# A second MoE's first product in 2x2 blocks: seven products for a pair of token tiles in place of eight

## The chip, the cores and the metric
The kernel runs on one core of a Trainium2 chip. The metric is the device time of one execution in microseconds (us), of which three runs of the kernel before were taken. A profile of one further execution shows what each engine did: TensorE (PE, with its weight loads as PEld), VectorE (DVE), ScalarE (ACT), GpSimd (POOL), and the DMA queue that SyncE issues (SP). [...]

## The reference
Linear attention without a softmax, a root-mean-square norm, and two MoE layers in a row, all in float32, on 4 x 576 = 2304 tokens of 512 channels:
```
out = q @ (k^T v) per head (8 heads of 64);  x = out / sqrt(mean(out^2) + 1e-6) * g_norm
y   = ((x @ w_a) * (x @ w_b)) @ w_out             # first MoE, d_ff 1536
h   = y @ w_in                                    # second MoE, 512 -> 1024
s   = h * softmax(h);  ln = (s - mean(s)) / sqrt(var(s) + 1e-6) * g_ln
out = ln @ w_out2                                 # 1024 -> 512
```
The weights come as float64. The change is about the product h.

## The kernel before
Each large matrix product is made of three TensorE products of rounded halves: both operands are split into a part hi that TensorE's float32 format (F32R) holds and a rest lo, and hi*hi + hi*lo + lo*hi are added up in PSUM (`three`, L562). A `group` is these three for one block of 128 along the summed axis.

**First stage.** For each of 12 slices f of 128 columns of d_ff, and each of 6 blocks j of 384 tokens, an *ab* item makes both products (24 matmuls of 384 columns), and ScalarE, VectorE and GpSimd turn them into the split gh and gl (L613 to L617); a *y* item (12 matmuls) multiplies them by w_out's slice, and VectorE adds the result to `ya`, y's sum in float32 (L657). Beside it the weights are decoded from float64 in chunks of 128 x 512 (`decode`, L275, five VectorE instructions), and `store` (L325) splits them: w_in into `winh` and `winl` with ScalarE and two GpSimd instructions a chunk, w_out2 later with g_ln's factor.

**Between the stages** `split_y` (L682) splits the whole of y into `yh` and `yl`, in the space that the first stage's x halves leave.

**Second stage**, for 18 token tiles of 128: `run_h` (L727) makes a tile's h (two banks of PSUM, a slot; 2 x 4 groups, 24 matmuls of 512 columns); `post_h` (L747) makes the softmax and the norm (reduce, exp, multiply, statistics, subtract); `run_t` (L783) transposes the result by 8 TensorE transposes and splits it into dh and dl; `run_o` (L808) is the output product (24 matmuls of 512 columns), scaled by ScalarE on the way out.

**The order** of instructions on every engine is fixed when the program is built. The class `Order` keeps a clock: `od.pe(cost, fn)` puts a TensorE piece and moves the clock on, `od.chain([...], rank, t)` puts a chain of steps on ACT ("A"), DVE ("V") and POOL ("G") as these come free by the stated costs, lower ranks first, without preemption. The engines then run in that order and wait on semaphores. Four PSUM slots of two banks each (`ps_tile`) serve ab, y, h, t and out in turn. While the first stage ends, a tile's h may run if no ab is left (L900); in the second stage a transpose goes first, then an h while fewer than four tiles are ahead of the outputs (`AHEAD`), then an output. All DMAs go through SP's queue in program order.

Of the kernel before, what the change touches and what calls it, by code (L numbers as in the profile page):

```python
# [113 lines left out]
def attention_moe_moe_kernel(ctx: ExitStack, tc, kv_in, kv_tail, q_in, g_norm, w1, w_in, w_out2, g_ln, out):  # L114
# [65 lines left out]
    extra = [("i", kt, n) for kt in range(NP) for n in range(2)] + [("o", x, 0) for x in range(3, NF2)]  # L180
# [5 lines left out]
    chunks += extra + [("o", x, 0) for x in range(3)]  # L186
# [68 lines left out]
    winh, winl, gwh, gwl, wf = {}, {}, {}, {}, {}  # L255
# [19 lines left out]
    def decode(k):  # L275
# [49 lines left out]
    def store(k, f, u, su, sf, t):  # L325

        what, x, y = k
        if what == "o" and x >= 3:
            wf[x] = w2.tile([P, CH], F32, tag=f"wf{x}", name=f"wf{x}", bufs=1)

            def keep():
                nc.gpsimd.tensor_tensor(out=wf[x], in0=f, in1=u, op=ALU.add)

            def kept(t):
                R_U.give(su)
                R_F.give(sf)
                scaled.append(x)
                decode_more()
                scale_more()

            od.chain([("G", 1.32, keep), (None, 0, kept)], rank=5, t=t)
            return
        if what == "i":
            if y == 0:
                winh[x] = w2.tile([P, DF2], F32R, tag=f"winh{x}", name=f"winh{x}", bufs=1)
                winl[x] = w2.tile([P, DF2], F32R, tag=f"winl{x}", name=f"winl{x}", bufs=1)
            hi, lo = (d[x][:, y * CH:(y + 1) * CH] for d in (winh, winl))
        elif R_WC.ok():
            hi, lo = wc[k] = take_wc(k)
        else:  # L350
            waiting.append((k, f, u, su, sf))
            return

        if what == "o":
            g = gl_sb[:, x:x + 1]
            gwh[x], gwl[x] = hi, lo
            ops = [
                ("G", 1.32, lambda: nc.gpsimd.tensor_tensor(out=f, in0=f, in1=u, op=ALU.add)),
                ("A", 0.6, lambda: nc.scalar.activation(out=hi, in_=f, func=AF.Copy, scale=g)),
                ("V", 0.66, lambda: nc.vector.scalar_tensor_tensor(  # L360
                    out=lo, in0=f, scalar=g, in1=hi.bitcast(F32), op0=ALU.mult, op1=ALU.subtract)),
            ]
        else:
            ops = [
                ("A", 0.58, lambda: nc.scalar.copy(out=hi, in_=f)),  # L365
                ("G", 1.32, lambda: nc.gpsimd.tensor_tensor(out=f, in0=f, in1=hi.bitcast(F32), op=ALU.subtract)),  # L366
                ("G", 1.32, lambda: nc.gpsimd.tensor_tensor(out=lo, in0=f, in1=u, op=ALU.add)),  # L367
            ]

        def done(t):  # L370
            R_U.give(su)
            R_F.give(sf)
            w_ready[k] = t
            decode_more()

        od.chain(ops + [(None, 0, done)], rank=rank_of(k) - 0.01, t=t)

    waiting, scaled = [], []

    def wc_used(k):  # L380

        R_WC.give(wc_slot[k])
        if waiting and R_WC.ok():
            store(*waiting.pop(0), od.now)
        scale_more()

    def scale_more():


        while scaled and not dec_q and not waiting:  # L390
            x = scaled[0]
            if x < 6:
                if not R_WC.ok():
                    return
                hi, lo = take_wc(("o", x, 0))
            elif ph2 is None:
                return
            else:
                hi, lo = (ph2.tile([P, CH], F32R, tag=f"gw{c}{x}", name=f"gw{c}{x}", bufs=1) for c in "hl")
# [3 lines left out]
    def scale(x, hi, lo):
        f, g = wf[x], gl_sb[:, x:x + 1]
        gwh[x], gwl[x] = hi, lo

        def done(t):
            w_ready["o", x, 0] = t

        od.chain([  # L410
            ("A", 0.6, lambda: nc.scalar.activation(out=hi, in_=f, func=AF.Copy, scale=g)),
            ("V", 0.66, lambda: nc.vector.scalar_tensor_tensor(
                out=lo, in0=f, scalar=g, in1=hi.bitcast(F32), op0=ALU.mult, op1=ALU.subtract)),
            (None, 0, done),
        ], rank=2)
# [208 lines left out]
    def y_items(fs, j):  # L624
# [10 lines left out]
        def run(f, m2, i):  # L635
# [15 lines left out]
            if i == 1 and f == fs[-1]:  # L651
# [7 lines left out]
                if m2 == 1:  # L659
                    ops.append((None, 0, lambda t: y_added(f, j)))  # L660
# [8 lines left out]
    yh, yl, y_ready = {}, {}, {}  # L669
    to_split = []  # L670
    POOL_SPLIT = (3, 4)

    def y_added(f, j):
        if f == NF1 - 1:
            to_split.append(j)
            split_more()

    def split_more():
        while to_split and all((NF1 - 1, to_split[0] // 3 * 3 + i) in ab_done for i in range(3)):
            split_y(to_split.pop(0))  # L680

    def split_y(j):  # L682
        hf, c0 = j // 3, (j % 3) * NB
        if j % 3 == 0:
            yh[hf] = xs.tile([P, NP, HALF], F32R, tag=f"xh{hf}", name=f"yh{hf}")
            yl[hf] = xs.tile([P, NP, HALF], F32R, tag=f"xl{hf}", name=f"yl{hf}")
        left = [2]
        e, cost, eng = ("G", 1.96, nc.gpsimd) if j in POOL_SPLIT else ("V", 0.87, nc.vector)

        def done(t):  # L690
            left[0] -= 1
            if not left[0]:
                y_ready[j] = t
                if j == NBLK - 1:
                    second()

        for i in range(2):
            src, dh, dl = (x[hf][:, 2 * i:2 * i + 2, c0:c0 + NB] for x in (ya, yh, yl))
            od.chain([
                ("A", 0.75, lambda dh=dh, src=src: nc.scalar.copy(out=dh, in_=src)),  # L700
                (e, cost, lambda dl=dl, dh=dh, src=src: eng.tensor_tensor(
                    out=dl, in0=src, in1=dh.bitcast(F32), op=ALU.subtract)),
                (None, 0, done),
            ], rank=1)
# [17 lines left out]
    todo_h, todo_t, todo_o = list(range(NTT)), list(range(NTT)), list(range(NTT))

    def h_ready(i):
        return max([y_ready.get(i // 3, INF), ps_ready()]) if R_H.ok() else INF

    def run_h(i):  # L727
        hf, c0 = i // 9, (i % 9) * P
        slot, ps = ps_tile(f"h{i}")
        sh = R_H.take()  # L730

        def group(n, kt):
            s = slice(n * 512, (n + 1) * 512)
            three(
                ps[:, n, :], yh[hf][:, kt, c0:c0 + P], yl[hf][:, kt, c0:c0 + P],
                winh[kt][:, s], winl[kt][:, s], kt == 0, kt == NP - 1,
            )

        for n in range(2):
            for kt in range(NP):  # L740
                od.pe(G2, lambda: group(n, kt))
        if ph2 is None:
            held.append(lambda: post_h(i, slot, ps, sh))
        else:
            post_h(i, slot, ps, sh)

    def post_h(i, slot, ps, sh):  # L747
        u = ph2.tile([P, 2, 512], F32, tag="u", name=f"u{i}", bufs=5)
# [21 lines left out]
        od.chain([  # L770
# [12 lines left out]
    def run_t(i):  # L783
# [4 lines left out]
        dh = ph2.tile([P, DF2], F32R, tag="dh", name=f"dh{i}", bufs=3)  # L788
        dl = ph2.tile([P, DF2], F32R, tag="dl", name=f"dl{i}", bufs=3)
# [70 lines left out]
    while any(ab) or busy or yq:  # L860
# [3 lines left out]
        if w2 is None and not att_left[0]:  # L864
# [4 lines left out]
            w2 = tc.alloc_tile_pool(name="w2", bufs=1, side="left", reuse_waits="tile")  # L869
            decode_more()  # L870
# [17 lines left out]
        if it:  # L888
# [8 lines left out]
            split_more()  # L897
# [13 lines left out]
    while todo_o:  # L911
        od.until(od.now)
        ahead = len(todo_o) - len(todo_h)
        h_can = todo_h and h_ready(todo_h[0]) <= od.now and (ph2 is not None or len(held) < 2)
# [8 lines left out]
        if h_can and (ahead < AHEAD or not o_can):  # L923
            run_h(todo_h.pop(0))
# [72 lines left out]
```

## Time and profile before
| what | us |
|---|---|
| median of 3 runs (lowest to highest) | 731.49 (730.91 to 731.96) |
| the profiled execution, its own time | 731.34 |
| its span, from the first to the last instruction | 729.6 |
| TensorE matmuls busy in the span | 713.9 (98%) |
| VectorE, ScalarE, GpSimd busy | 492.2, 245.6, 282.7 |

The profiled execution's time is the span and 1.7 us around it. Matmuls overlap, so the duration in a row (0.39 us for 512 columns) is longer than the distance between two starts; costs of TensorE are read from starts. Idle time "<- X" was ended by X.

### The profile page before, as it was taken

The page shows a single profiled execution, that of the slowest core. Times are in us where ns is not written, and L with a number is a line of the kernel's source. Part 1 is how long each engine was busy: PE and PEld are TensorE (multiplying, and loading weights), DVE is VectorE, ACT ScalarE, POOL GpSimd, SP SyncE. Part 2 cuts the span into 40 slices and gives each one's busy share as a digit, 9 for nine tenths or more (in the row PEclk, how much of TensorE's full clock was granted, in tenths as well). Part 3 has the DMA queues.
Part 4 walks back from the last instruction along what each step waited for, and adds up shares of the span by engine and source line. Part 5 has one row for each costly group of instructions (what it writes and reads, how often), then busy time and mean ns, then how long its engine had stood idle before and what let it go on. Part 6 is the DMA issues. An engine that isn't in the chain of part 4 may idle for free.

```text
span 729.6 us, 10425 instructions
## 1 busy us (share of the span) xinstructions
PE 713.9 (98%) x4184; PEld 669.5 (92%) x4184; DVE 492.2 (67%) x674; ACT 245.6 (34%) x458; POOL 282.7 (39%) x271
## 2 busy tenths in 40 slices
PE   6889999999999999999999999999999999999998
PEld 5779999999999999999999999999878888888887
DVE  3999557797979796969694848457784453635450
ACT  4767544323333332222222222224432121222221
POOL 2876445655556464444444343222421111111010
PEclk9999999999999999999999999999999999999999
DMA  8951501121212121212121200000000000000001
GB/s 309 336 214 60 181 1 58 58 88 58 87 57 86 42 83 52 95 50 87 59 71 46 88 0 30 1 1 1 0 1 30 29 16 30 15 30 15 29 30 44
DMA packets 16336, 46.81 MB, mean 64 GB/s; under 512 B 2080, under 2 KB 3360, under 8 KB 16288
## 3 DMA queue, kind: packets, MB, share of 16 engines
q1 hardware_dynamic: 16288, 46.15, 17.8%
q8 instruction: 33, 0.54, 0.3%
q14 instruction: 15, 0.12, 0.1%
HBM read 41.42 MB, written 4.72 MB: 63 GB/s over the span
## 4 chain that ended last, share of the span: by engine, by line
PE 92%; DMA 3%; DVE 2%; ACT 1%; SPq 1%; issue 0%; ACTq 0%
PE y L644 20%; PE ab L563 13%; PE ab L564 13%; PE ab L565 13%; PE h L563 5%; PE h L565 5%; PE out L565 5%; PE out L563 5%; PE out L564 4%; PE h L564 4%; PE t L793 2%; DMA tail<-in_kv_tail 1%; PE o L491 1%; PE pkv L468 1%; DMA raw_w<-in_w 1%; PE t L533 1%
## 5 line engine op out<-in xcount | busy, mean ns | idle before, releaser
L563 PE MATMUL ab<-xh,wh_w 128*128 128x384 f32 x576 | 194.5, 338 | 0.0
L564 PE MATMUL ab<-xl,wh_w 128*128 128x384 f32 x576 | 192.6, 334 | 0.3 <-DVE xl L547 0.3
L565 PE MATMUL ab<-xh,wl_w 128*128 128x384 f32 x576 | 192.5, 334 | 0.0
L617 POOL TENSOR_TENSOR gl<-a,gh 128x384 fp32r<-128x384 f32 x72 | 77.7, 1079 | 190.4 <-ACT gh L616 190.2
L657 DVE TENSOR_TENSOR ya<-y,ya 128x768 f32<-128x768 f32 x132 | 125.2, 952 | 8.0 <-PE y L644 5.1
L563 PEld LDWEIGHTS ab<-xh,wh_w 128*128 128x128 f32 x576 | 108.2, 188 | 0.9 <-issue 0.3
L564 PEld LDWEIGHTS ab<-xl,wh_w 128*128 128x128 f32 x576 | 108.2, 188 | 0.6 <-DVE xl L547 0.6
L565 PEld LDWEIGHTS ab<-xh,wl_w 128*128 128x128 f32 x576 | 108.1, 188 | 0.0
L614 DVE TENSOR_TENSOR a<-ab,a 128x384 f32<-128x384 f32 x72 | 40.0, 555 | 88.5 <-ACT a L613 88.5
L644 PE MATMUL y<-gh,wh_w 128*128 128x384 f32 x288 | 96.9, 336 | 0.0
L644 PE MATMUL y<-gh,wl_w 128*128 128x384 f32 x288 | 96.3, 334 | 0.0
L644 PE MATMUL y<-gl,wh_w 128*128 128x384 f32 x288 | 96.2, 334 | 0.0
L613 ACT COPY a<-ab 128x384 f32<-128x384 f32 x72 | 34.4, 478 | 130.6 <-PE ab L565 130.6
L771 DVE TENSOR_REDUCE st<-h 128x1 f32<-128x1024 f32 x18 | 22.0, 1221 | 67.1 <-PE h L565 67.0
L366 POOL TENSOR_TENSOR f_w<-f_w,wh_w 128x512 f32<-128x512 f32 x36 | 48.6, 1349 | 38.1 <-ACT wh_w L365 38.1
L563 PE MATMUL h<-winh,yh 128*128 128x512 f32 x144 | 56.2, 390 | 0.8 <-DVE u L773 0.8
L565 PE MATMUL h<-winh,yl 128*128 128x512 f32 x144 | 56.2, 390 | 0.0
L564 PE MATMUL h<-winl,yh 128*128 128x512 f32 x144 | 56.1, 389 | 0.0
L644 PEld LDWEIGHTS y<-gh,wh_w 128*128 128x128 f32 x288 | 54.1, 188 | 0.3 <-issue 0.2
L644 PEld LDWEIGHTS y<-gl,wh_w 128*128 128x128 f32 x288 | 54.1, 188 | 0.0
L644 PEld LDWEIGHTS y<-gh,wl_w 128*128 128x128 f32 x288 | 54.1, 188 | 0.0
L367 POOL TENSOR_TENSOR wl_w<-f_w,u_w 128x512 fp32r<-128x512 f32 x36 | 51.7, 1436 | 1.8
(92 smaller groups left out, 1141.7 us busy)
## 6 DMA issues: line engine op xcount, KB each, us to landing
raw_w<-in_w SPq DMA_DIRECT2D x36, 512.0 KB, 3.3
kv<-in_kv SPq DMA_DIRECT2D x16, 512.0 KB, 5.2
out<-ot SPq DMA_DIRECT2D x17, 256.0 KB, 2.0
raw_i<-in_w_in SPq DMA_DIRECT2D x8, 512.0 KB, 3.3
raw_o<-in_w_out SPq DMA_DIRECT2D x8, 512.0 KB, 3.2
q<-in_q SPq DMA_DIRECT2D x12, 288.0 KB, 6.0
tail<-in_kv_tail SPq DMA_DIRECT2D x4, 256.0 KB, 6.5
q<-in_q SPq DMA_DIRECT2D x4, 192.0 KB, 4.9
```

The costliest lines, as they stand in the source:

```text
L366: ("G", 1.32, lambda: nc.gpsimd.tensor_tensor(out=f, in0=f, in1=hi.bitcast(F32), op=ALU.subtract)),
L367: ("G", 1.32, lambda: nc.gpsimd.tensor_tensor(out=lo, in0=f, in1=u, op=ALU.add)),
L563: nc.tensor.matmul(o, lhsT=ah, rhs=bh, start=first, stop=False)
L564: nc.tensor.matmul(o, lhsT=ah, rhs=bl, start=False, stop=False)
L565: nc.tensor.matmul(o, lhsT=al, rhs=bh, start=False, stop=last)
L613: ("A", 0.45, lambda: nc.scalar.copy(out=a, in_=ps[:, 0, 0:NB])),
L614: ("V", 0.5, lambda: nc.vector.tensor_tensor(out=a, in0=ps[:, 1, 0:NB], in1=a, op=ALU.mult)),
L617: ("G", 0.96, lambda: nc.gpsimd.tensor_tensor(out=gl, in0=a, in1=gh.bitcast(F32), op=ALU.subtract)),
L644: nc.tensor.matmul(o, lhsT=x[:, s], rhs=y, start=f == fs[0] and n == 0, stop=f == fs[-1] and n == 2)
L657: op = ("V", 0.87, lambda: nc.vector.tensor_tensor(out=dst, in0=src, in1=dst, op=ALU.add))
L771: ("V", 1.13, lambda: nc.vector.tensor_reduce(out=nmax, in_=ps, axis=AX.XY, op=ALU.max, negate=True)),
L793: nc.tensor.transpose(ps[:, ft * P:(ft + 1) * P], u[:, ft * P:(ft + 1) * P], ident)
```

## The change
y is cut for each pair of token tiles into 2x2 blocks (rows: the two tiles; columns: the first and second 256 channels), w_in into 2x2 blocks of 256 x 512. The pair's h is then made of seven block products P1 to P7 (Winograd's form of Strassen's method) of 6 matmuls each, of 512 columns. Four of them take sums of blocks of y (S1 to S4), four take sums of blocks of w_in (T1 to T4). The results are combined in PSUM: ScalarE copies P1 to `s1` and P5 to `s5`; VectorE adds s1 to P6 in place, P7 is accumulated on that, VectorE writes V from it and s5, P4 is accumulated on Y, P3 on P5, and VectorE adds s1 (by then overwritten with P1 + P6) to Z.

w_in's sums are made while the first stage runs (`sums`), for the first half of the channels of each block (g = 0) and then the second (g = 1); six of g = 0's seven operands are written to HBM and read back at the end of the first stage into the space of the x halves (`late_loads`). w_out2's chunks are all scaled and split when they are decoded, in their raw buffer, written to HBM and read back as well. y is not split as a whole: `ya` stays, and `make_a` makes S1 to S4 on VectorE and the splits on ScalarE and GpSimd for each pair. Rings get smaller (R_H 5 to 4, R_D 3 to 2). The diff, cut:
```diff
-    extra = [("i", kt, n) for kt in range(NP) for n in range(2)] + [("o", x, 0) for x in range(3, NF2)]
+    extra = [("i", kt, n) for k in range(2) for kt in (k, k + 2) for n in range(2)]
+    extra += [("o", x, 0) for x in range(NF2)]
...
-            R_RAW.give(slot)
+            if k[0] != "o":
+                R_RAW.give(slot)
...
+        if what == "i":
+
+            g, r = x % 2, 2 * (x // 2) + y
+            if g and len(made[0]) < 7:
+                waiting_i.append((k, f, u, su, sf))
+                return
+
+            def have(t):
+                free()
+                there[g].add(r)
+                sums(g)
+
+            od.chain([("G", 1.32, lambda: nc.gpsimd.tensor_tensor(out=bt[:, r], in0=f, in1=u, op=ALU.add)),
+                      (None, 0, have)], rank=5, t=t)
             return
...
+        if what == "o":
+
+            g = gl_sb[:, x:x + 1]
+            at = raw.bitcast(F32R)
+            hi, lo = at[:, 0:CH], at[:, CH:2 * CH]
+
+            def out_to(t):
+                free()
+                d = scr["o", x] = dr.tile([P, 2 * CH], F32, tag=f"so{x}", name=f"so{x}")
+                nc.sync.dma_start(out=d, in_=raw.bitcast(F32))
+                scr_at["o", x] = when = od.load(8 * CH * P) + 1.5
+                od.chain([(None, 0, gone)], t=when)
+
...
+            od.chain([
+                ("G", 1.32, lambda: nc.gpsimd.tensor_tensor(out=f, in0=f, in1=u, op=ALU.add)),
+                ("A", 0.7, lambda: nc.scalar.activation(out=hi, in_=f, func=AF.Copy, scale=g)),
+                ("V", 0.85, lambda: nc.vector.scalar_tensor_tensor(
+                    out=lo, in0=f, scalar=g, in1=hi.bitcast(F32), op0=ALU.mult, op1=ALU.subtract)),
+                (None, 0, out_to),
+            ], rank=5, t=t)
+            return
...
+    def sums(g):
+        b11, b12, b21, b22, ta, tb = (bt[:, i] for i in range(6))
+
+        def sub(o, a, b):
+            return ("G", 1.35, lambda: nc.gpsimd.tensor_tensor(out=o, in0=a, in1=b, op=ALU.subtract))
+
+        def pair(n, src):
+            at = wd[0 if (g, n) == (0, 6) else n + 1]
+            hi, lo = at[:, 0:CH], at[:, CH:2 * CH]
+
+            def done(t):
+                if g == 0 and n < 6:
+                    d = scr["i", n] = dr.tile([P, 2 * CH], F32, tag=f"si{n}", name=f"si{n}")
+                    nc.sync.dma_start(out=d, in_=at.bitcast(F32))
+                    scr_at["i", n] = od.load(8 * CH * P) + 1.5
+                else:
+                    bop[g, n], b_at[g, n] = (hi, lo), t
+                made[g].add(n)
+                if waiting_i and len(made[0]) == 7:
+                    for w in waiting_i:
+                        store(*w, t)
+                    waiting_i.clear()
+
+            return [("A", 0.6, lambda: nc.scalar.copy(out=hi, in_=src)),
+                    ("G", 1.35, lambda: nc.gpsimd.tensor_tensor(out=lo, in0=src, in1=hi.bitcast(F32), op=ALU.subtract)),
+                    (None, 0, done)]
+
+        parts = [
+            ({0}, lambda: pair(B11, b11)),
+            ({0, 1}, lambda: [sub(ta, b12, b11)] + pair(T1, ta)),
+            ({2}, lambda: pair(B21, b21)),
+            ({0, 1, 2, 3}, lambda: pair(B22, b22) + [sub(tb, b22, b12)] + pair(T3, tb) + [sub(b12, b22, ta)]
+             + pair(T2, b12) + [sub(ta, b21, b12)] + pair(T4, ta)),
+        ]
+        for i, (need, ops) in enumerate(parts):
+            if i not in begun[g] and need <= there[g] and (i < 3 or T1 in made[g]):
+                begun[g].add(i)
+                more = [(None, 0, lambda t: sums(g))] if i == 1 else []
+                od.chain(ops() + more, rank=5, t=od.now)
...
+    def late_loads():
+
+        for c in range(2):
+            if c not in late and all((NF1 - 1, j) in ab_done for j in range(3 * c, 3 * c + 3)) and len(made[0]) == 7:
+                late[c] = [xs.tile([P, 4 * HALF], F32R, tag=f"x{d}{c}", name=f"late{d}{c}") for d in "hl"]
+                for i, n in enumerate(((B11, T2, B21, T1), (B22, T3))[c]):
+                    at = late[c][1][:, i * 1024:i * 1024 + 1024]
+                    nc.sync.dma_start(out=at.bitcast(F32), in_=scr["i", n])
+                    bop[0, n], b_at[0, n] = (at[:, 0:CH], at[:, CH:]), max(od.load(8 * CH * P), scr_at["i", n] + 2)
+                a_more()
...
+            late["o", x] = True
+            gwh[x], gwl[x] = hi, lo
+            for c, o in enumerate((hi, lo)):
+                nc.sync.dma_start(out=o.bitcast(F32), in_=scr["o", x][:, c * CH:(c + 1) * CH])
+            w_ready["o", x, 0] = max(od.load(8 * CH * P), scr_at["o", x] + 2)
...
+            y_ready[j] = t
+            a_more()
+            if len(y_ready) == NBLK:
+                second()
...
+    R_H, R_D, R_AO = Ring(4), Ring(2), Ring(2)
...
+    AT = {"A11": 0, "A12": 1, "A22": 2, "S1": 3, "S2": 4, "S3": 5, "S4": 6}
+    SEQ = [("P1", "A11", B11), ("P6", "S2", T2), ("P2", "A12", B21), ("P5", "S1", T1), ("P7", "S3", T3),
+           ("P3", "S4", B22), ("P4", "A22", T4)]
...
+    def a_more():
+
+        while todo_a and R_AO.ok() and R_AO.taken % 2 in late and max(
+                y_ready.get(j, INF) for j in range(NBLK) if j in (2 * todo_a[0] // 3, (2 * todo_a[0] + 1) // 3)) < INF:
+            i = todo_a.pop(0)
+            make_a(i, R_AO.take(), max(y_ready[2 * i // 3], y_ready[(2 * i + 1) // 3]))
...
+    def make_a(i, slot, when):
+        at = late[slot % 2][0]
...
+        def add(o, a, b, op):
+            return ("V", 0.4, lambda: nc.vector.tensor_tensor(out=o, in0=a, in1=b, op=op))
+
+        def part(cost, d, src, last):
+            n = slice(*d)
+
+            def done(t):
+                left[0] -= 1
+                if not left[0]:
+                    a_ops[i] = t, at, slot
+
+            od.chain([
+                ("A", cost, lambda: nc.scalar.copy(out=hi[:, n], in_=src)),
+                ("G", 2.2 * cost, lambda: nc.gpsimd.tensor_tensor(
+                    out=lo[:, n], in0=src, in1=hi[:, n].bitcast(F32), op=ALU.subtract)),
+                (None, 0, done),
+            ], rank=2.5, t=max(od.now, last))
+
+        left = [4]
+        part(0.6, (0, 2), first, when)
+        part(0.35, (2, 3), a22.unsqueeze(1), when)
+        od.chain([
+            add(s[:, 0], a21, a22, ALU.add), add(s[:, 1], s[:, 0], a11, ALU.subtract),
+            (None, 0, lambda t: part(0.6, (3, 5), s[:, 0:2], t)),
+            add(s[:, 2], a11, a21, ALU.subtract), add(s[:, 3], a12, s[:, 1], ALU.subtract),
+            (None, 0, lambda t: part(0.6, (5, 7), s[:, 2:4], t)),
+        ], rank=2.5, t=max(od.now, when))
...
+    def next_h():
+
+        if not hp:
+            i = todo_h[0] // 2 if todo_h else None
+            if (i not in a_ops or R_H.taken - len(R_H.given) > 2
+                    or sum(t <= od.now for t in ps_free.values()) < 2):
+                return INF
+            return max([a_ops[i][0]] + [b_at.get((g, B11), INF) for g in range(2)])
+        p = hp[0]
+        name, _, n = SEQ[p["n"]]
+        t = max(b_at.get((g, n), INF) for g in range(2))
+        need = {"P2": "s1", "P7": "u2", "P3": "s5", "P4": "v"}.get(name)
+        return max(t, p.get(need, INF)) if need else t
...
+        name, s, n = SEQ[p["n"]]
+        (_, p1), (_, p2) = p["slots"]
+        X, Z, Y, V = p1[:, 0], p1[:, 1], p2[:, 0], p2[:, 1]
+        o = {"P1": X, "P2": X, "P5": Z, "P3": Z, "P6": Y, "P7": Y, "P4": Y}[name]
+        a = p["a"]
+        for k in range(2):
+            c = AT[s] * 256 + k * P
+            ah, al = a[:, c:c + P], a[:, c + 1792:c + 1792 + P]
+            bh, bl = bop[k, n]
+
+            first = name in ("P1", "P5", "P6")
+
+            def group():
+                for m, (x, y) in enumerate(((ah, bh), (ah, bl), (al, bh))):
+                    nc.tensor.matmul(o, lhsT=x, rhs=y, start=first and k == m == 0, stop=k == 1 and m == 2,
+                                     skip_group_check=not first)
+
+            od.pe(G2, group)
...
+        s1, s5 = bt[:, 4], bt[:, 5]
+        at = od.now + 0.2
...
+        def try_v(t):
+            if "p7" in p and "s5" in p and "v0" not in p:
+                p["v0"] = True
+                od.chain([("V", 0.69, lambda: nc.vector.tensor_tensor(out=V, in0=Y, in1=s5, op=ALU.add)), is_done("v")],
+                         rank=1, t=t)
+
+        if name == "P1":
+            od.chain([("A", 0.6, lambda: nc.scalar.copy(out=s1, in_=X)), is_done("s1")], rank=1, t=at)
+        elif name == "P6":
+            def go(t):
+                if "s1" not in p:
+                    od.chain([(None, 0, go)], t=t + 0.2)
+                    return
+                od.chain([("V", 0.69, lambda: nc.vector.tensor_tensor(out=Y, in0=Y, in1=s1, op=ALU.add)),
+                          ("A", 0.6, lambda: nc.scalar.copy(out=s1, in_=Y)), is_done("u2")], rank=1, t=t)
+            od.chain([(None, 0, go)], t=at)
+        elif name == "P5":
+            od.chain([("A", 0.6, lambda: nc.scalar.copy(out=s5, in_=Z)), is_done("s5")], rank=1, t=at)
+        elif name == "P7":
+            od.chain([is_done("p7")], t=at)
+        elif name == "P3":
+            pre = [("V", 0.69, lambda: nc.vector.tensor_tensor(out=Z, in0=Z, in1=s1, op=ALU.add))]
+            post_or_hold(p["i"], p["slots"][0], p["u"][0], pre)
+        elif name == "P4":
+            R_AO.give(p["sa"])
+            hp.pop()
+            post_or_hold(p["i"] + 1, p["slots"][1], p["u"][1], [])
+            a_more()
+
+    def post_or_hold(i, slot, sh, pre):
...
-        od.chain([
+        od.chain(pre + [
...
-        dh = ph2.tile([P, DF2], F32R, tag="dh", name=f"dh{i}", bufs=3)
-        dl = ph2.tile([P, DF2], F32R, tag="dl", name=f"dl{i}", bufs=3)
+        dh = ph2.tile([P, DF2], F32R, tag="dh", name=f"dh{i}", bufs=2)
+        dl = late[sd % 2][0][:, 3584:3584 + DF2]
...
+            wd = [w2.tile([P, 2 * CH], F32R, tag=f"wd{n}", name=f"wd{n}") for n in range(8)]
+            bt = w2.tile([P, 6, CH], F32, tag="bt", name="bt")
...
-        if todo_h and not busy and not any(ab) and len(yq) <= 2 and h_ready(todo_h[0]) <= od.now and len(held) < 2:
-            run_h(todo_h.pop(0))
+        if not busy and not any(ab) and len(todo_h) > NTT - 2 + 2 * (not hp) and next_h() <= od.now:
+            run_h()
             continue
...
-        h_can = todo_h and h_ready(todo_h[0]) <= od.now and (ph2 is not None or len(held) < 2)
+        h_can = next_h() <= od.now
...
-        if h_can and (ahead < AHEAD or not o_can):
-            run_h(todo_h.pop(0))
+        if h_can and (hp or ahead < AHEAD or not o_can):
+            run_h()
```

## Rows read from the trace of the kernel before

**Rows 1.** The page's busy times, shares and instruction counts of the engines
```profile
PE 713.9 (98%) x4184; PEld 669.5 (92%) x4184; DVE 492.2 (67%) x674; ACT 245.6 (34%) x458; POOL 282.7 (39%) x271
```

**Rows 2.** Busy time by stretch: length, then PE, PEld, DVE, ACT, POOL; granted clock
```profile
18.00:27.00 9.00, 7.01 (x74) 5.18 (x74) 8.15 (x15) 7.25 (x19) 6.75 (x5) 1.00 0.82 299
...
152.50:190.00 37.50, 37.50 (x218) 37.50 (x217) 31.55 (x44) 11.97 (x22) 20.36 (x16) 1.00 0.20 71
...
600.00:640.00 40.00, 40.00 (x191) 33.37 (x190) 20.50 (x26) 9.11 (x13) 6.58 (x15) 1.00 0.06 22
```

**Rows 3.** Groups of instructions by line and shape: busy us, mean ns of one
```profile
L563 PE MATMUL h<-winh,yh 128*128 128x512 f32 x144 | 56.2, 390 | 0.8 <-DVE u L773 0.8
```

**Rows 4.** Timeline of PE in the second stage: start, duration
```profile
602.60 0.39 PE L563 MATMUL h<-winh,yh 128*128 128x512 f32 x1
...
608.05 1.04 PE L793 MATMUL t<-ident,u 128*128 128x128 f32 x8
...
614.38 0.39 PE L563 MATMUL h<-winh,yh 128*128 128x512 f32 x1
```

**Rows 5.** Timeline of DVE in the second stage, one tile
```profile
608.32 1.22 DVE L771 TENSOR_REDUCE st<-h 128x1 f32<-128x1024 f32 x1 [5.21 <-PE h L565]
610.18 1.23 DVE L803 TENSOR_TENSOR dl<-t,dh 128x1024 fp32r<-128x1024 f32 x1 [0.63 <-ACT dh L802]
611.32 1.22 DVE L773 TENSOR_TENSOR u<-h,u 128x1024 f32<-128x1024 f32 x1
612.57 1.29 DVE L754 BATCH_NORM_STATS2 st<-u 128x6 f32<-128x512 f32 x2
...
614.14 0.75 DVE L776 TENSOR_SCALAR u<-u,st 128x1024 f32<-128x1024 f32 x1
```

**Rows 6.** Groups by line and shape, nearest in kind to the added instructions
```profile
L366 POOL TENSOR_TENSOR f_w<-f_w,wh_w 128x512 f32<-128x512 f32 x36 | 48.6, 1349 | 38.1 <-ACT wh_w L365 38.1
...
L292 DVE TENSOR_SCALAR u_w<-u_w 128x512 uint32<-128x512 uint32 x36 | 19.1, 530 | 0.3
...
L547 DVE SCALAR_TENSOR_TENSOR xl<-t,gn,xh 128x512 fp32r<-128x512 f32 x16 | 11.9, 744 | 2.1 <-ACT xh L546 1.9
...
L508 ACT COPY x<-o 128x512 f32<-128x512 f32 x16 | 9.5, 592 | 0.0
...
L292 DVE TENSOR_SCALAR u_i<-u_i 128x512 uint32<-128x512 uint32 x8 | 9.1, 1134 | 0.1
...
L547 DVE SCALAR_TENSOR_TENSOR xl<-t,gn,xh 128x256 fp32r<-128x256 f32 x4 | 1.9, 480 | 3.3 <-ACT xh L546 3.2
```

**Rows 7.** Timeline of PE at the first stage's end
```profile
508.33 0.33 PE L565 MATMUL ab<-xh,wl_w 128*128 128x384 f32 x1
...
510.58 0.39 PE L563 MATMUL h<-winh,yh 128*128 128x512 f32 x1
...
516.06 0.33 PE L644 MATMUL y<-gh,wh_w 128*128 128x384 f32 x1
```

**Rows 8.** Timeline of ACT and POOL there
```profile
509.88 0.47 ACT L613 COPY a<-ab 128x384 f32<-128x384 f32 x1
...
511.40 0.52 ACT L616 CAST gh<-a 128x384 fp32r<-128x384 f32 x1 [0.31 <-DVE a L614]
...
510.06 3.69 POOL L701 TENSOR_TENSOR yl<-ya,yh 128x768 fp32r<-128x768 f32 x2 [4.83 <-ACT yh L700]
513.68 1.04 POOL L617 TENSOR_TENSOR gl<-a,gh 128x384 fp32r<-128x384 f32 x1
```

**Rows 9.** Waits of PE, by what ended them: total us, times, longest
```profile
PE h L563 <- DVE u L773: 0.8, 1, 0.8
```

**Rows 10.** Timeline of PE at the start, two of the same product
```profile
5.48 1.12 PE L468 MATMUL pkv<-kv 128*64 128x64 f32 x16 [5.48 <-DMA kv<-in_kv]
...
23.11 0.69 PE L468 MATMUL pkv<-kv 128*64 128x64 f32 x16 [0.17 <-ACT x L508]
```

**Rows 11.** The page's DMA issues: KB each, median us from issue to landing
```profile
raw_w<-in_w SPq DMA_DIRECT2D x36, 512.0 KB, 3.3
```

More of the change, by code (lines that the diff above doesn't have):

```diff
@@ L185, in attention_moe_moe_kernel @@
             extra = extra[2:]
-    chunks += extra + [("o", x, 0) for x in range(3)]
+    chunks += extra
     a_loads = []
@@ L323, in decode, with store, free @@
         )
-    def store(k, f, u, su, sf, t):
+    def store(k, f, u, su, sf, t, slot=None, raw=None):
         what, x, y = k
[L328 to L342, printed above, removed]
-        if what == "i":
[L344 to L351, printed above, removed]
+        def free():
+            R_U.give(su)
+            R_F.give(sf)
+            decode_more()
+        if what == "i":
+            g, r = x % 2, 2 * (x // 2) + y
[8 more added lines that the diff above has]
+                      (None, 0, have)], rank=5, t=t)
             return
@@ L370, in done @@
+            return
+        if not R_WC.ok():
+            waiting.append((k, f, u, su, sf))
+            return
+        hi, lo = wc[k] = take_wc(k)
         def done(t):
-            R_U.give(su)
-            R_F.give(sf)
             w_ready[k] = t
-            decode_more()
-        od.chain(ops + [(None, 0, done)], rank=rank_of(k) - 0.01, t=t)
-    waiting, scaled = [], []
+            free()
+        od.chain([
+            ("A", 0.58, lambda: nc.scalar.copy(out=hi, in_=f)),
+            ("G", 1.32, lambda: nc.gpsimd.tensor_tensor(out=f, in0=f, in1=hi.bitcast(F32), op=ALU.subtract)),
+            ("G", 1.32, lambda: nc.gpsimd.tensor_tensor(out=lo, in0=f, in1=u, op=ALU.add)),
+            (None, 0, done),
+        ], rank=rank_of(k) - 0.01, t=t)
@@ L403, in scale @@
[L403 to L408, printed above, removed]
-        od.chain([
[L411 to L415, printed above, removed]
+    late = {}
+    def late_loads():
[7 more added lines that the diff above has]
+                a_more()
+        for x in range(NF2):
+            if ("o", x) in late or scr_at.get(("o", x), INF) > od.now:
+                continue
+            if x >= 6:
+                if 1 not in late:
+                    continue
+                at = late[1][1][:, (x - 4) * 1024:(x - 3) * 1024]
+                hi, lo = at[:, 0:CH], at[:, CH:]
+            elif any(k[0] == "w" for k in dec_q) or waiting or any(
+                    k[0] == "w" and k not in w_ready for k in list(arrived) + list(wc)) or not R_WC.ok():
+                continue
+            else:
+                hi, lo = take_wc(("o", x, 0))
+            late["o", x] = True
[3 more added lines that the diff above has]
+            w_ready["o", x, 0] = max(od.load(8 * CH * P), scr_at["o", x] + 2)
@@ L666, in y_items, with y_added @@
         ]
[L669 to L673, printed above, removed]
+    y_ready = {}
+    def y_added(f, j, t):
         if f == NF1 - 1:
[L675 to L704, printed above, removed]
+            y_ready[j] = t
+            a_more()
+            if len(y_ready) == NBLK:
+                second()
     def second():
         nonlocal ph2
-        assert not dec_q and not waiting
-        yp.release()
+        assert not dec_q and not waiting and not waiting_i
         ph1.release()
@@ L715, in second @@
         held.clear()
-        scale_more()
-    R_H, R_D = Ring(5), Ring(3)
+    R_H, R_D, R_AO = Ring(4), Ring(2), Ring(2)
     held, d_ready, dt_ready, scs = [], {}, {}, {}
     G2 = 0.68
[L722 to L741, printed above, removed]
+    todo_a, todo_h, todo_t, todo_o = list(range(NTT // 2)), list(range(NTT)), list(range(NTT)), list(range(NTT))
```

77 lines of the change are left out of this document (42 added, 35 removed).

## Prediction
> **What bounds the kernel now.** I read the page's engine shares first: PE is busy for 98% of the span, the next engine, DVE, for 67% [rows 1]. A share is an average, so I went to the stretches: in one slice of the first stage and in the second stage PE is busy all the time, at a granted clock of 1.00, while DVE has 6 us of 37.5 free in the first and half of the time in the second [rows 2]. The list of waits then has only one of PE in the second stage, 0.8 us, for a PSUM slot [rows 9]. So the time is the sum of TensorE's instructions, and what is taken from them shortens it as long as the others keep up.
>
> What one costs is read from starts. Tile after tile, a group of 24 h matmuls takes 608.05 - 602.60 = 5.45 us, 0.227 us each, transposes and output 614.38 - 608.05 = 6.33, together 11.78 us a tile [rows 4]. (The 390 ns of the grouped row [rows 3] overlap.) 18 tiles have 432 such matmuls, three groups of 144 [rows 3].
>
> **What the change removes.** Nine pairs with 7 x 6 matmuls make 378; 54 fall away, 54 x 0.227 = 12.3 us. All else on TensorE stays. From the profiled execution, 731.34 us: 719.1, if nothing new is exposed. That execution lies 0.15 us under the median, so I forecast the median by the same number.
>
> [...]
>
> **The first stage's end: +1.6 us.** Before, the wait for the last y item is filled with h: ab ends at 508.33 + 0.17 = 508.5, y of the item before runs until 510.58, then a whole h until the last y at 516.06 [rows 7]. The new condition that lets h in there is `len(todo_h) > NTT - 2 + 2 * (not hp)`: with no pair begun it reads 18 > 18, and a pair can only begin there. So nothing covers the last y. Its chain is 0.27 us from TensorE's end to the reader (an h's end 608.05 to its reduce 608.32 [rows 4, 5]), 2.04 from the copy's start to gh's end with 0.47 of that waiting for DVE, gl 1.04 [rows 8], and about 0.3 of hand-offs: 3.2 us, less y's 2.08 (510.58 - 508.5) = 1.1. gl came only at 513.68 because GpSimd was in split_y's 3.69 us [rows 8]; that goes, but make_a's splits for pair 1 are let in just then, and one of them (1.35, nearest row [rows 6]) may stand in front of gl. I take 1.6, bounds 1.1 and 3.0.
>
> **What must have arrived: 0.** Four operands are read back when the third ab of the last slice is done, three ab and y items (36 matmuls of 37.5/218 = 0.172 us each [rows 2], 6.2) ahead of the end, 18.6 us; one after another at 3.3 us each [rows 11] they need 13.2. T3, the last of the two later ones, lands 6.6 us after 508.5 = 515.1 and is read by the pair's fifth product, at about 514.2 + 4 x 1.36 = 519.6. If w_out2's loads stand ahead of them in SP's queue, it is some us late, once; that is in the range.
>
> **Pairs 0 and 1: +2.0 us.** There is no output yet to put between. After pair 0 (9.5 us) pair 1 follows; pair 0's first tile has its last product 1.36 before its end, then VectorE and ScalarE need an add 0.74, reduce 1.22, exp as long as the reduce of its shape, 1.2 (an estimate), multiply 1.25, statistics 1.57, subtract 0.75 [rows 5, 6], 6.7 alone, interleaved with the other tile's 6 and pair 1's three adds and pair 2's four sums (0.74 and 0.48 each [rows 6]). The first transpose falls into pair 1; the second and the first dl come about 1.6 us after it is over. With some 1.2 of waits inside pair 1 and less the 0.8 that PE waits there now [rows 9]: +2.0, bounds 0 and 6.
>
> **Seven later pairs: +2.5 us.** A pair has four short waits: P2 for s1's copy (0.27 + 0.59 + 0.1 = 0.96, behind P6's 1.36), P7 for add and copy (1.8, behind 2.7), P3 for s5's copy (0.96 behind 1.36), P4 for V (0.27 + 0.74 + 0.1 = 1.11 behind 1.36) [rows 4 to 6]. Undisturbed all are hidden, with 0.25 to 0.9 to spare; but DVE and ACT take what came first, and a reduce is 1.22. Its load per pair: twice 5.94 (1.22 + 1.14 + 1.25 + 1.57 + 0.75, by starts [rows 5]) = 11.9, three adds 2.2, four sums 1.9: 16.0 of 22.2 us (2 x 11.78 - 6 x 0.227), 72% in place of half. Where the order foresees a late operand it puts an output product (5.45) first, and in the steady order (pair, out, t, out, t) one or two are ready. I take 0.35 us a pair, 2.5 in all; bounds 0 and 1.2 a pair (an op of 1.22 begun just before), 8.4.
>
> The row for contention: the same VectorE instruction takes 530 ns on the first stage's weights and 1134 on w_in's chunks [rows 6], so something on the chip can double it. [...]
>
> **The first stage: 0.** w_in's eight chunks cost GpSimd 16 instructions, now 8 adds, 8 sums and 14 splits: 14 more, 19 us [rows 6], over four slices, 20.4 + 4.7 = 25.1 of 37.5 each [rows 2], 28.5 in the slice where g = 0's last four are due. [...] Scales of w_out2 (0.74 each, two a slice) come there from later. The weights' ring holds two slices, so a late chunk has a slice to catch up. SP's stores wait for splits with the weight loads behind them: same cover; DMA is used to 0.20 [rows 2]. Bounds 0 and 3.
>
> **Sum:** 731.34 - 12.3 + 1.6 + 2.0 + 2.5 = 725.1; all lower bounds 719.1 + 1.1 = 720.2, all upper ones 719.1 + 3.0 + 6 + 8.4 + 3 = 739.5, which won't meet.
>
> **Rivals.**
> *VectorE is late in every pair* (12%). [...] For it: DVE's 72% and the doubled rows. Against it: output products stand ready to fill.
>
> *PSUM slots: slower* (11%). A pair takes two of four slots at once and holds them until both softmaxes have multiplied. If the next pair comes up with one output as cover, it waits for the second tile: about 7.5 us after P4, less 5.45 = 2.0, over eight starts 16: 719.1 + 1.6 + 16 = 736.7. It decides from (12.3 - 1.6) / 8 = 1.3 us a start. For it: even now, with one slot a tile, the only wait is for a slot [rows 9]. Against: a pair's slots are held 13 and 17 us, two t 3.5 each, two outputs 6.4 each, 50 of 4 x 22.2 = 89 slot-us.
>
> *The clock falls* (2%). At the start the same product takes 1.12 us after a wait of 5.48 and 0.69 later [rows 10], though the granted clock reads full. Were PE's gaps inside pairs to do this, nine pairs at 1.62 times would add 9 x 9.5 x 0.62 = 53: 778. Against it: between 18 and 27 us PE was busy 7.01 of 9 at 1.00 [rows 2]. [...]
>
> *The first stage becomes VectorE's* (4%): each of the four w_in slices 1.5 over: 731.
>
> *As forecast* (71%): 720 to 729, faster.
>
> Within 0.2% (1.5 us) of 731.5, about what a measurement of this kernel can tell, lie half of the first rival and most of the last: faster 0.81, same 0.07, slower 0.12. The range for 8 in 10 is 720.2 to 731: the lower bounds' sum to the first rival.
>
> **What would show it.** In the second stage a steady period of about 22.5 us for two tiles with 378 h matmuls; PE idle of 1 to 3 us before the last y; PE's waits on DVE and ACT inside pairs near 0.35 us each; DVE at 70 to 80% there. I would be wrong if PE waited over 1.3 us a pair for slots or V, if PE's first-stage windows lost their 100%, or if the read-back operands were waited for.

## The result, and the profile after

| | median us | lowest to highest, runs | ratio to before, 95% |
|---|---|---|---|
| before | 731.73 | 730.91 to 732.04, 4 | |
| changed | 722.87 | 722.29 to 723.49, 4 | 0.9881 (0.9864 to 0.9898) |
| changed, once more beside before's 731.82 | 722.37 | 722.08 to 722.77, 4 | 0.9863 (0.9844 to 0.9881) |

The change takes 8.9 us off, where 6.4 were forecast (725.1 from 731.5). The page's shares first:
```profile
span 720.7 us, 10567 instructions
...
PE 701.9 (97%) x4130; PEld 658.4 (91%) x4130; DVE 522.6 (73%) x729; ACT 272.6 (38%) x515; POOL 333.1 (46%) x317
```
PE has 54 instructions less than in [rows 1], 4184 - 4130, and is still the busiest. DVE has 55 more and is busy 30 us longer in a shorter span. By stretches, with the columns of [rows 2]; the first two lie in the first stage, the others from its end on:
```profile
227.50:265.00 37.50, 37.47 (x217) 37.15 (x216) 33.69 (x49) 12.89 (x24) 23.71 (x20) 1.00 0.24 83
...
302.50:340.00 37.50, 37.47 (x216) 37.15 (x215) 33.86 (x50) 13.09 (x24) 18.62 (x16) 1.00 0.28 99
...
510.00:530.00 20.00, 18.81 (x88) 15.68 (x87) 12.14 (x16) 8.83 (x17) 8.06 (x9) 1.00 0.49 165
524.00:538.00 14.00, 12.89 (x65) 10.34 (x64) 13.88 (x20) 7.26 (x13) 6.12 (x11) 1.00 0.00 0
538.00:552.00 14.00, 14.00 (x70) 11.84 (x71) 13.87 (x20) 6.79 (x11) 6.42 (x11) 1.00 0.11 39
560.00:640.00 80.00, 80.00 (x382) 66.82 (x382) 55.47 (x83) 35.85 (x59) 29.82 (x47) 1.00 0.07 24
```
Three things are to be seen. Two windows of the first stage have a PEld that is no longer full: 0.35 us is missing in each (before, it reads 37.50 in both). From 524 to 552 DVE is busy 99% of the time. And later, 560 to 640, PE is full again while DVE is at 69%, on the average of 80 us. The waits of PE from 480 us on:
```profile
PE out L624 <- DVE lateh L945: 1.1, 1, 1.1
PE y L705 <- POOL gl L678: 1.0, 1, 1.0
PE y L705 <- ACT gh L677: 0.2, 1, 0.2
```
None of them is one of an h product. The idle time of a row is counted to the modelled end of the matmul before; what a wait costs is the distance of starts. The starts on PE around these waits, to be held against [rows 7] and [rows 9]:
```profile
509.54 0.33 PE L626 MATMUL ab<-xh,wl_w 128*128 128x384 f32 x1
...
512.20 0.45 PE L705 MATMUL y<-gh,wh_w 128*128 128x384 f32 x1 [0.24 <-ACT gh L677]
...
513.60 0.44 PE L705 MATMUL y<-gl,wh_w 128*128 128x384 f32 x1 [0.95 <-POOL gl L678]
...
535.79 1.07 PE L935 MATMUL t<-ident,u 128*128 128x128 f32 x8
537.96 0.50 PE L624 MATMUL out<-wh_o,dh 128*128 128x512 f32 x1 [1.10 <-DVE lateh L945]
```
Before, PE's one wait:
```profile
534.54 1.91 PE L793 MATMUL t<-ident,u 128*128 128x128 f32 x16
537.24 0.47 PE L563 MATMUL h<-winh,yh 128*128 128x512 f32 x1 [0.79 <-DVE u L773]
```
After, the last y item but one ends twelve matmuls after 509.71, at 511.79; the last y starts 0.41 later, its second matmul 1.23 later than due, its third 0.11: 1.74 us. Eight transposes take 0.80, so the first output was due at 536.59 and starts 1.37 late. The one wait of before costs, counted so, 1.10 (from 534.54, two times 0.80, and the h at 537.24).

A steady pair is one of 22.20 us: in the chain of work that ended last, two blocks of 42 h matmuls begin so far apart.
```profile
655.59 9.54 PE h L843 x42
...
677.79 9.54 PE h L843 x42
```

**A measure for the experiments.** The first 100 us, the attention, end at another time in each profile: its last transposes start at 99.26 and 98.89 in two profiles of before, and between 98.87 and 100.49 in eleven of the changed kernel and its variants. So besides the medians I give D, from the start of the last ab matmul (509.54) to the start of the last copy out (717.57): 208.03 us here, 208.09 in the second profile; before 218.02 and 218.03. Two profiles of one kernel differ in D by 0.06 us at most. The medians hold one more thing that D leaves out: the time outside the span is 1.7 to 1.9 us in ten of the thirteen profiles, but 2.1 in both of the changed kernel and in that of its first variant below.

### The profile page after: what moved, and what is told of

Its sections match the earlier page's. It is cut to its first block, busy times and chain, and to the rows that moved or that the text cites. A ratio compares the mean times of both kernels' runs of the same rounds, so it can differ in the third digit from the quotient of the medians.

```text
span 720.7 us, 10567 instructions
## 1 busy us (share of the span) xinstructions
PE 701.9 (97%) x4130; PEld 658.4 (91%) x4130; DVE 522.6 (73%) x729; ACT 272.6 (38%) x515; POOL 333.1 (46%) x317
## 4 chain that ended last, share of the span: by engine, by line
PE 90%; DVE 3%; DMA 3%; ACT 1%; POOL 1%; issue 1%; SPq 0%; ACTq 0%
PE y L705 20%; PE ab L624 14%; PE ab L625 13%; PE ab L626 13%; PE h L843 10%; PE out L624 5%; PE out L626 5%; PE out L625 5%; DMA kv<-in_kv 2%; PE t L935 2%; PE o L552 2%; PE pkv L529 1%; DMA tail<-in_kv_tail 1%; PE t L594 1%; ACT sq L577 0%
## 5 line engine op out<-in xcount | busy, mean ns | idle before, releaser
L678 POOL TENSOR_TENSOR gl<-a,gh 128x384 fp32r<-128x384 f32 x72 | 75.9, 1054 | 150.0 <-ACT gh L677 149.9
L718 DVE TENSOR_TENSOR ya<-y,ya 128x768 f32<-128x768 f32 x132 | 123.4, 949 | 2.8 <-PE y L705 1.0
L843 PE MATMUL h<-wd,lateh 128*128 128x512 f32 x216 | 58.6, 391 | 0.0
L677 ACT CAST gh<-a 128x384 fp32r<-128x384 f32 x72 | 36.8, 512 | 41.9 <-DVE a L675 41.3
L389 POOL TENSOR_TENSOR wl_w<-f_w,u_w 128x512 fp32r<-128x512 f32 x36 | 50.7, 1407 | 2.9 <-DVE u_w L309 1.4
L843 PEld LDWEIGHTS h<-wd,lateh 128*128 128x128 f32 x216 | 40.3, 188 | 8.3
L843 PE MATMUL h<-latel,lateh 128*128 128x512 f32 x162 | 46.3, 394 | 0.0
```

What stands on the lines that cost most here:

```text
L677: ("A", 0.45, lambda: nc.scalar.copy(out=gh, in_=a)),
L678: ("G", 0.96, lambda: nc.gpsimd.tensor_tensor(out=gl, in0=a, in1=gh.bitcast(F32), op=ALU.subtract)),
L718: op = ("V", 0.87, lambda: nc.vector.tensor_tensor(out=dst, in0=src, in1=dst, op=ALU.add))
L843: nc.tensor.matmul(o, lhsT=x, rhs=y, start=first and k == m == 0, stop=k == 1 and m == 2, skip_group_check=not first)
```

## The experiments

| kernel | median us | before beside it | ratio, 95% | D |
|---|---|---|---|---|
| pair 0 before the last y | 721.00 | 731.64 | 0.9855 (0.9840 to 0.9870) | 206.39 |
| eight products | 733.26 | 731.64 | 1.0026 (1.0016 to 1.0035) | 219.17 |
| no output within pairs | 722.63 | 731.64 | 0.9873 (0.9858 to 0.9888) | 208.32 |
| V twice, not planned | 727.08 | 731.64 | 0.9936 (0.9919 to 0.9952) | 213.09 |
| V twice, planned | 725.77 | 732.28 | 0.9912 (0.9895 to 0.9928) | 210.93 |
| dl first | 721.77 | 732.28 | 0.9859 (0.9845 to 0.9874) | 207.40 |
| both | 719.93 | 732.28 | 0.9834 (0.9819 to 0.9848) | 205.73 |
| V twice in pairs 2 to 8 | 724.11 | 731.90 | 0.9890 (0.9872 to 0.9907) | 209.72 |
| V twice in pairs 0 and 1 | 723.85 | 731.90 | 0.9884 (0.9865 to 0.9904) | 209.28 |

**Pair 0 before the last y.** The condition that can't become true is mended:
```diff
-        if not busy and not any(ab) and len(todo_h) > NTT - 2 + 2 * (not hp) and next_h() <= od.now:
+        if not busy and not any(ab) and (hp or len(todo_h) == NTT) and next_h() <= od.now:
```


> Theory A (the time is TensorE's sum; the last y item was left uncovered): with pair 0 let in before the last y, the 1.2 us of TensorE's wait there goes, 1.2 us less than the changed kernel: 721.7, no wait of y for gl in the trace. Rival B (the last y's delay is absorbed later, since VectorE bounds the first 14 us of the second stage and the first output waits for it anyway): 722.9, the wait at the first output grows from 1.1 to about 2.3 us.

D is 1.64 us shorter, and the waits of PE from 480 us on are down to one line:
```profile
PE out L624 <- DVE lateh L945: 1.1, 1, 1.1
```
P1 and P6 now stand between the last two y items. The first output's wait has not grown: theory A, with nearly the 1.74 us that starts show, not the 1.2 of the idle column. The delay was the last y's alone.

**Eight products.**
```diff
-        for k in range(2):
+        for k in (0, 1, 0, 1) if name == "P1" else (0, 1):
```


> P1 is made twice (its second run starts anew and writes the same values), so that a pair has eight products again with all the rest of the change. Theory A: 54 more matmuls of 0.227 us, +12.3 us, 735.1, some 3.4 us slower than the kernel before: that is the price of all the rest of the change. Rival B (VectorE or the waits inside pairs set the pair's pace): the added product is hidden in part, under +8 us, 731 or less.

D grows by 11.14 us. The extra product also fills time in front of the first output:
```profile
536.76 1.62 PE L843 MATMUL h<-wd,lateh 128*128 128x512 f32 x6
538.65 0.50 PE L624 MATMUL out<-wh_o,dh 128*128 128x512 f32 x1 [0.27 <-DVE lateh L945]
```
From 536.76 the six h matmuls are due to end after 1.36 us, and the output starts after 1.89, 0.53 late. In the changed kernel P4, the transposes behind it and the output are 0.26 + 1.37 = 1.63 late. So 1.1 us are filled, and the 54 matmuls cost 12.2, as worked out. By medians the kernel with eight products is 1.6 us slower than before (0.16 to 0.35%), not 3.4. Of the difference 1.1 is what the extra product fills, and 0.35 lies outside the span of the profiled runs. Rival B is out.

**No output within pairs.**
```diff
-        if o_can:
+        if o_can and not hp:
             run_o(todo_o.pop(0))
```


> No output product may start between the seven products of a pair. Theory A (pairs have no waits because an output product stands in where a product is late): TensorE waits inside most pairs, about 0.5 us each and more where a posted softmax is in front, +3 to +7 us, 726 to 730. Rival B (the pair's own products hide the copies and adds, the output in between is chance): within 1 us of 722.9.

D is 0.29 us longer, the median the same within 0.3, and the list of PE's waits is that of the changed kernel, with none at an h product. The changed kernel puts an output into three pairs (from 553.5, 617.8 and 641.4 us on). Without it P2 of pair 2 starts 0.3 us late, which is all of the 0.29; the two others lose nothing. Theory A falls but for that pair: the pair's own products hide its copies and adds.

**V twice**, first behind the planner's back, then with its knowledge:
```diff
-                od.chain([("V", 0.69, lambda: nc.vector.tensor_tensor(out=V, in0=Y, in1=s5, op=ALU.add)), is_done("v")],
-                         rank=1, t=t)
+                add_v = lambda: nc.vector.tensor_tensor(out=V, in0=Y, in1=s5, op=ALU.add)
+                od.chain([("V", 0.69, lambda: (add_v(), add_v())), is_done("v")], rank=1, t=t)
```
The second run has 1.38 in place of 0.69.


> The add that makes V runs twice in a row (the same values), and the order's clock isn't told: 0.7 us more on VectorE in each pair, and P4 has to wait for it where P3 alone stands before it (0.25 us to spare by the working of the prediction). Theory A (hidden with little to spare): +0.45 us in the pairs in which nothing else stands between P3 and P4, +1 to +4 us in all. Rival B (VectorE bounds the second stage): +0.7 us in each of nine pairs, +6.3 us. Rival C (VectorE has much to spare): +0.

> As the run with V added twice, but the order's clock counts both (1.38 us), so that another piece can be put before P4. Theory A: within 0.5 us of the changed kernel, 722.9 to 723.4, no waits of h for V. Rival B (VectorE bounds the second stage): +6.3 us again.

Not planned, D grows by 5.06. P4 waits for V in five pairs, as here:
```profile
567.23 0.84 PE L843 MATMUL h<-wd,lateh 128*128 128x512 f32 x3
568.31 1.66 PE L843 MATMUL h<-wd,lateh 128*128 128x512 f32 x6 [0.24 <-DVE h L857]
```
By starts each of these waits costs 0.51 us, 0.24 by the idle column. So 0.2 of the added 0.70 is hidden, near the 0.25 to spare that the prediction worked out, and theory A holds for these five. What it left out is the rest: pair 1's second transposes are 0.73 later than in the changed kernel, waiting for the normalized tile, and the clock falls once (to 0.57 from 540 to 544 us, which costs 1.6, see the last section). Planned, D grows by 2.90, where A had 0.5 at most and B 6.3. The waits of P4 in pair 0 and of pair 1's transposes stay, and others come; two more runs separate early pairs from late ones.

**V twice in a part of the pairs**, planned, with `p["i"] >= 4` or `p["i"] < 4`:
```diff
...
+                n_v = 2 if p["i"] >= 4 else 1
+                od.chain([("V", 0.69 * n_v, lambda: [add_v() for _ in range(n_v)]), is_done("v")], rank=1, t=t)
```


> V is added twice, with the order's clock told, in pairs 2 to 8 only. V twice in all nine pairs cost 2.9 us of TensorE's time from the last ab matmul to the last copy out. Theory D (VectorE is the bound only for the first 28 us of the second stage, pairs 0 and 1, and has time to spare afterwards): +0.7 us at most over the changed kernel. Rival B (VectorE bounds every pair a little): 7 of the 9 shares, +2.3 us.

> V is added twice, with the order's clock told, in pairs 0 and 1 only. Theory D: the two adds, 2 x 0.7 = 1.4 us, and the wait that they bring are paid here, +1.4 to +2.3 us. Rival B: 2 of the 9 shares, +0.6 us.

Late adds cost 1.69 us, early ones 1.25; together 2.94, the planned run's 2.90. The early ones are paid in two places: P4 of pair 0 waits 0.5 for V, as unplanned, since the order has nothing else to put there, and the second transposes of pair 1 come 0.73 late, in the stretch where DVE is full (13.88 of 14 us above). The late ones are not paid evenly, 0.24 a pair, as the sum suggests. Of PE with V twice in pairs 2 to 8:
```profile
591.73 0.84 PE L843 MATMUL h<-wd,lateh 128*128 128x512 f32 x3
593.25 0.50 PE L624 MATMUL out<-wh_o,dh 128*128 128x512 f32 x1 [0.69 <-DVE lateh L946]
...
635.30 0.94 PE L843 MATMUL h<-latel,lateh 128*128 128x512 f32 x3
...
657.50 0.94 PE L843 MATMUL h<-latel,lateh 128*128 128x512 f32 x3
```
An output that the order puts into pair 4 comes 0.84 late for its dl, and P7 of pairs 3 and 5 by 0.27 and 0.29: 1.4 of the 1.69. From pair 6 on nothing is paid: the pairs that begin at 635.30 and 657.50 are 22.20 us apart, as without the added step. The 69% of DVE from 560 to 640 is an average over full stretches and half idle ones. A window of the changed kernel, then two of this run:
```profile
566.00:580.00 14.00, 14.00 (x67) 11.63 (x66) 13.93 (x20) 7.49 (x14) 6.21 (x11) 1.00 0.00 1
```
```profile
580.00:594.00 14.00, 13.31 (x67) 10.75 (x66) 13.69 (x17) 6.83 (x11) 6.00 (x8) 1.00 0.05 19
...
635.30:657.50 22.20, 22.20 (x109) 18.57 (x108) 16.82 (x24) 9.48 (x17) 7.86 (x12) 1.00 0.07 24
```
Neither theory holds as put. Theory D is right that the later pairs have time to spare, but they have it from pair 6 on, not from pair 2.

**dl first**, and both edits:
```diff
             ps_done(slot),
             (None, 0, done),
-        ], rank=2, t=od.now + 0.2)
+        ], rank=1, t=od.now + 0.2)
```


> The split of a transposed tile (dh, dl) is ranked before softmax steps. Theory A (the first output waits 1.1 us because a reduce of pair 1 was put before the first dl on VectorE, and nothing else covers it): that wait goes, 1.1 us less than the changed kernel, 721.8. Rival B (VectorE is the bound in those 14 us, what is moved back is waited for instead): 722.9, a wait of the same size at a neighbouring place.

> Pair 0 before the last y, and dl ranked first. Theory A: both waits gone, 2.3 us less than the changed kernel, 720.6. Rival B (VectorE bounds the start of the second stage): 721.7 to 722.9, with 1 to 2 us of waits left there.

dl first shortens D by 0.63, less than the output's wait of 1.37: the wait is gone from the list, but by starts the first output is still 0.24 late, and P2 of pair 2, in front of which the changed kernel has an output, loses 0.5 on ScalarE's copy (rival B in part). Both together shorten D by 2.30, the sum of 1.64 and 0.63: at 719.93 us the fastest version, 0.9834 of before. One short wait, that of P2, is left from 480 us on:
```profile
PE h L843 <- ACT bt L861: 0.2, 1, 0.2
```

**Before and changed once more**


> The kernel before, profiled once more: the 1.2 us by which the changed kernel's first stage ended later is either the scatter of the first loads' landing (then this profile's last ab matmul starts up to 1.2 us later than 508.33 as well) or a cost of the early sums (then it starts within 0.3 us of 508.33).

> The changed kernel, profiled once more, with more timed rounds: by scatter of the first loads the last ab matmul starts anywhere between 508.3 and 510.2, and the distance from there to the last copy out stays at 207.7 us within 0.2; the ratio to the kernel before stays in 0.986 to 0.990.

The kernel before takes 731.85 us this time, beside 731.82. Its last ab matmul starts at 507.96, 0.37 earlier than in the first profile, which neither reading foresaw; the changed kernel's, at 509.14, and its distance from there (D unchanged within 0.06) and its ratio lie as expected. From the attention's last transposes to the last ab matmul are 409.07 us in both profiles of before, and 409.70 and 409.72 in the changed kernel's: 0.6 us of the 1.2 are a cost of the first stage. The other part lies ahead of 100 us. There the eleven profiles of the changed kernel and its variants reach from 98.87 to 100.49, 99.75 on average, and before's two are 98.89 and 99.26; whether that is scatter alone stays open.

## Why the prediction was right, and where its terms were off

**The 12.3 us: right.** The run with eight products gives 12.2, 0.226 us for each of the 54 matmuls. The 227 ns of [rows 4] holds.

**The last y: +1.6 predicted, 1.74 measured.** The step was right as it stood: the condition lets nothing in, and GpSimd's split for pair 1 stands in front of gl. ACT and POOL there:
```profile
510.44 0.47 ACT L674 COPY a<-ab 128x384 f32<-128x384 f32 x1
510.61 1.98 POOL L790 TENSOR_TENSOR lateh<-ya,lateh 128x512 fp32r<-128x512 f32 x2 [4.18 <-ACT lateh L789]
...
511.64 0.51 ACT L677 CAST gh<-a 128x384 fp32r<-128x384 f32 x1
...
512.55 0.99 POOL L678 TENSOR_TENSOR gl<-a,gh 128x384 fp32r<-128x384 f32 x1
```
gh ends at 512.15; gl starts at 512.55, when the two splits are through: about 0.4 of the 1.74. Before, it was split_y's 3.69 us that stood there [rows 8].

**What must have arrived: 0, right.** No wait of PE for a DMA is in the list after 100 us. T3 landed at 515.94, where 515.1 was worked out, some 5 us before it was read.

**Pairs 0 and 1: +2.0 predicted, 0.53 measured.** The first output is 1.37 late (1.6 was worked out), P4 of pair 1 and the start of the transposes behind it take 0.26 longer than six matmuls (1.62 from 534.17, where 1.36 are due), of which 0.10 is no wait, since the first matmuls behind transposes are about that much longer in the steady pairs too (three from 595.08 on take 0.78 in place of 0.68) and before (one at 608.85 takes 0.31 in place of 0.23); I had 1.2 for waits inside pair 1. And the wait of before that goes is worth 1.10 by starts, not 0.8. The mechanism, VectorE behind while no output is there yet, is shown by DVE's 99% there and by the 0.73 us that the early adds cost there.

**Seven later pairs: +2.5 predicted, 0 measured.** The slack that the step worked out (0.25 to 0.9 us) is enough by itself; the reason that it gave besides, that an output stands in, counts for 0.3 us in pair 2 and nothing later, by the run without outputs in pairs. How near the edge it is, V twice shows: unplanned, 0.70 us more on VectorE costs P4 0.51; planned, it costs up to pair 5, and nothing in the steady pairs 6 to 8.

**The first stage: 0 predicted, 0.6 measured.** The bound of 0 to 3 held, but one of the prediction's own signs of being wrong showed faintly: PE has 37.47 of 37.50 us in two windows. The weak rival had the mechanism right: VectorE gets late. One of two like places (the other is at 303 us), 0.3 us each, on ACT, DVE, POOL and PE:
```profile
222.29 0.48 ACT L674 COPY a<-ab 128x384 f32<-128x384 f32 x1 [1.64 <-PE ab L626]
...
223.19 1.32 POOL L389 TENSOR_TENSOR wl_w<-f_w,u_w 128x512 fp32r<-128x512 f32 x1 [0.72 <-DVE u_w L309]
223.39 1.67 DVE L300 SCALAR_TENSOR_TENSOR f_i<-raw_i,u_i 128x512 uint32<-128x512 uint32 x1
...
226.16 0.55 DVE L675 TENSOR_TENSOR a<-ab,a 128x384 f32<-128x384 f32 x1
...
227.58 1.01 POOL L678 TENSOR_TENSOR gl<-a,gh 128x384 fp32r<-128x384 f32 x1
...
228.28 0.34 PE L705 MATMUL y<-gh,wh_w 128*128 128x384 f32 x1
228.65 0.45 PE L705 MATMUL y<-gl,wh_w 128*128 128x384 f32 x1
```
The copy of a is through at 222.77, but VectorE multiplies it only at 226.16, after decode steps of up to 1.7 us; gl ends 0.3 us after y's first matmul starts. The long step runs beside GpSimd's split of a first-stage weight (L389), which the kernel before has too, and not beside an early sum; at 303 us it is the same, with a chunk of w_out2. VectorE's five steps on w_in take 33.4 us in all, 36.0 before. So the rows do not bear out that the early sums make these steps longer; what put a chunk's steps in front of the multiply stays open.

**The sum.** -12.26 + 1.74 + 0.53 + 0 + 0.62 = -9.37, from 731.34: 721.97. The profiled execution took 722.87; the attention's end lay 0.58 later, and what lies behind the start of the last copy, with the time outside the span, was 0.31 longer, which makes 722.86. The forecast of 725.1 was 2.2 us above the median. The two terms for pairs were 4.0 too high together; the last y and the first stage, 0.8 too low, and the 0.9 outside the sum made up for part of that, which is luck.

**The rivals.** PSUM slots: no wait for one is left in the list, not even that of [rows 9]; the pair's two slots were no bound. VectorE late in every pair: not in the changed kernel, and with 0.7 us more of it only up to pair 5. The 731 to which the range goes was an estimate for this rival, and no run shows a load of VectorE that leads to it: from 560 to 640 us it is busy 55.47 of 80 us, PE 80.00. The clock: 1.00 in every stretch shown of the changed kernel; it fell once in a variant (below). Counted from its list of rivals, the prediction's chances are about 0.78 for faster and 0.13 for slower, not 0.81 and 0.12; nothing hangs on it.

## What to carry to other kernels

Where one engine is busy all the time, count what leaves it by the distance of starts, and then look for each place where the new order has nothing to put before a late operand: here the end of a stage and the first pieces of the next cost more than all the steady ones. A short slack that the products themselves give, worked out from rows, held here; a run that adds one dummy step prices it, and its cost is read place by place, since an average over pairs, like a busy share over 80 us, hid that pairs 3 to 5 paid nearly all and the steady ones nothing. A condition in a hand-written order is worth evaluating with its starting values: one that could never be true cost 1.64 us here.

## What the runs showed of the hardware that I had not expected

**The clock fell once, behind two short waits.** With V twice and not planned, PE waits 0.73 and 1.11 us within 3 us in front of the first output. Two windows of that run, then the same two of the run with V twice in pairs 0 and 1, columns as in [rows 2]:
```profile
536.00:540.00 4.00, 2.16 (x14) 1.45 (x13) 3.96 (x7) 2.66 (x5) 3.35 (x4) 1.00 0.00 0
540.00:544.00 4.00, 4.00 (x11) 3.14 (x12) 3.94 (x5) 2.20 (x4) 0.41 (x2) 0.57 0.02 4
```
```profile
536.00:540.00 4.00, 2.16 (x14) 1.45 (x13) 4.00 (x6) 2.66 (x5) 2.63 (x6) 1.00 0.00 0
540.00:544.00 4.00, 4.00 (x19) 3.32 (x18) 3.94 (x5) 1.92 (x4) 1.14 (x4) 1.00 0.01 4
```
In the first run the granted clock is 0.57 on the average of 540 to 544 us, and eight matmuls start 0.43 us apart in place of 0.227, some 1.6 us; in the second, and in the planned run of nine pairs, PE is idle in front of the first output for as long, 1.84 of 4 us, and the clock stays at 1.00. What decides between them stays open. The prediction's clock rival did not come in the changed kernel; what it feared was seen once, behind two waits of about a microsecond, close together.

**VectorE beside GpSimd's splits.** Of the changed kernel's 36 adds of two 128 x 256 operands, 29 took VectorE 0.37 to 0.43 us; two took 1.5 while GpSimd was splitting; DVE, then POOL:
```profile
547.95 1.52 DVE L778 TENSOR_TENSOR bt<-bt,ya 128x256 f32<-128x256 f32 x1
549.39 1.50 DVE L778 TENSOR_TENSOR bt<-ya 128x256 f32<-128x256 f32 x1
550.81 0.41 DVE L778 TENSOR_TENSOR bt<-ya,bt 128x256 f32<-128x256 f32 x1
...
547.76 2.84 POOL L790 TENSOR_TENSOR lateh<-bt,lateh 128x512 fp32r<-128x512 f32 x2
```
GpSimd's two splits end at 550.60; the add that starts after them takes 0.41. Five more adds began while GpSimd was splitting and took 0.55 to 1.00 us, the longest at 653.74. What makes them longer, the trace does not show. The 0.48 that the prediction took for such an add was between the two.
